# A short expert's tile, the third full tile and the two counts moved into the straight part of an attention, FFN and routed-FFN kernel

## The chip, the cores and the metric

The kernel runs on one core of one Trainium2 chip. The metric is the device time of one execution in microseconds (us), taken as the median of several runs. One core has five engines that work beside each other, each in the order of its own instructions: TensorE (PE, matmuls and transposes), VectorE (DVE), ScalarE (ACT), GpSimd (POOL) and SyncE (SP), and 16 DMA engines that the queues of SP and POOL feed. They wait for each other through semaphores.

## What is computed

The reference, cut to what matters:

```python
# q, k, v: 4 x 8 x 576 x 64, omega: 128 x 64
x = attention_by_random_features(q, k, v, omega)      # 2304 tokens x 512
x = (silu(x @ w_gate) * (x @ w_val)) @ w_out          # 512 -> 1536 -> 512

do_compute = x @ w_skip > 0                           # tokens that are routed
e_idx = np.argmax(x[do_compute] @ w_gate2, axis=1)    # one of 8 experts
for e in range(8):                                    # gate_w: softmax value of e
    h = np.maximum(xc[mask] @ w1[e], 0.0)             # 512 -> 1024
    y[mask] = gate_w[mask, None] * (h @ w2[e])        # 1024 -> 512
out[do_compute] = xc + y                              # the others: out = x
```

All is in fp32, which the kernel keeps by splitting each operand in a high and a low part and multiplying three times (high x high, low x high, high x low). For these inputs the routing sends 576 tokens to expert 1, 1135 to expert 5 and 2 to expert 4.

## The kernel before

**Order of the work.** The program is written by a small list scheduler, the class `Order` (the object `od`). A task is a Python generator that yields steps `op(engine, ns, cells it must wait for, take=(slots it needs))`. `od.run()` always takes the step that can start first by its own clock (ties by priority, the second argument of `od.add`) and emits its instructions then. So the order of instructions on each engine comes out of those estimates; on the chip every engine then follows that order, and semaphores make it wait for data. A `Cell` (`C["pick", 1]`, `C["mload", 2]`, ...) holds the time by which a step is done; slots are buffers: `hp` three PSUM banks for the up-projection of the second FFN, `y` two for its down-projection, `raw` landing buffers for weights, `ys` for copies of results.

**Stages.** Attention and the first FFN fill the program up to about 614 us and run on in part beside the routed FFN. This one works in tiles of `TS` = 288 tokens of one expert. Tiles 0 and 1 (`m` = 0, 1) are chosen early, from all but the last tokens (`early_pick`). The rest is chosen by `late_pick` (L945) after the last token is routed: a table of 64 pairs (expert, tile) with its count of tokens in each; DVE's MAX8 and FIND_INDEX8 sort out the 16 fullest (`ix[1]`, experts in `ei[1]`), and a second list (`ix[2]`, `ei[2]`) holds the "short" pairs of at most `FEW` = 64 tokens. `m2["ti"]` gets two counts: how many short pairs and how many full ones. Here they are 1 and 4 (tiles 2 to 5).

**One full tile** (`m2_tile`, L1388): `m2_up` 96 matmuls in 8 groups `fc` of 12, each into one `hp` bank (the first six of group 0 are issued ahead by `m2_head`), `m2_hidden` after each group (ACT writes the relu, L1161, DVE the low part, L1163, and the bank is free), `m2_down` 4 groups of 24 matmuls in triples (L1178 to L1180), transposed back through `yt` (L1191), scaled and added on DVE (L1202) and scattered to `out` by POOL (L1217). For the next tile it fetches the list `ids` (`m2_ids`, SP, L1042 and L1043, three landing buffers), gathers rows with POOL (`m2_gather`, L1053), transposes them (`m2_tr`, L1114; copies and low parts in L1121 to L1123), loads eight weight pieces of 0.5 MB on SP (`m2_load`, L1088) and splits each in two steps of ACT (L1099) and DVE or POOL (L1101) (`m2_split`). Weights of tile `m` lie in `W[m % 2]`.

**One short tile** (`s_*`): 64 tokens, with the tokens as the stationary side. `s_load` (L1232) and `s_split` (L1245) bring its weights into `W[1]`, `s_tokens` its list (L1256, L1257) and its rows (L1262), `s_turn` transposes them (L1293). `s_tile` runs two halves of 8 matmuls (L1319), each followed by `s_hidden` (ACT and DVE copy L1355, PE transposes L1365, ACT and DVE L1369 to L1377), then 16 matmuls (L1331) and a scatter. It holds one `hp` and both `y` banks (`s_banks`), given back by `s_back`.

**The border.** The straight program has tiles 0 and 1, the preparations of tile 2, and the loads, the first half of the split and the transposes of short tile 0. Then every engine reads the two counts into registers (`values_load`, L1510 and L1511), a nest of `tc.If(few > s)` holds up to eight short tiles (L1512), and a nest of `tc.If(cnt > n)` tiles 2 to 16 (L1525).

## Time and profile before

| | us |
|---|---|
| three runs | 860.98, 861.69, 858.26 |
| median | 860.98 |
| the profiled execution | 858.62 |
| its span from first to last instruction | 856.8 |
| PE busy in the span | 826.3 (96%) |
| DVE, ACT, POOL busy | 519.0, 446.0, 213.4 |
| mean granted clock of TensorE | 0.988 of full speed |

All times of rows are from the profiled execution and count from the start of its span. Busy time of PE is modelled from its pipelined matmuls. A timeline row gives start, duration, engine, line, operation, output and inputs, and how often it repeats; in brackets stands how long the engine was idle before and what released it. "PEldq", "SPq" and so on are the sequencers of the engines, which issue DMAs, take branches and load registers; these don't count as busy. PEclk is the clock that the throttle granted TensorE, 1.00 being full speed.

### The profile page before, as it was taken

What the parts mean: (1) busy time and instruction counts of PE and PEld (TensorE: products, weight loads), DVE (VectorE), ACT (ScalarE), POOL (GpSimd) and SP (SyncE); (2) the same over time, 40 slices, a digit from 0 to 9 for tenths busy, and PEclk for the clock granted to TensorE, in tenths of its full rate; (3) what the DMA queues carried; (4) which work ended last, traced back from release to release, by engine and by line L of the source; (5) the groups of instructions that cost most, each with busy time, mean ns of one, the idle gap of its engine ahead of it and who ended that gap; (6) DMA issues with size and microseconds to landing.
All of it is one profiled execution on the core that took longest, in us unless ns stands there. A gap on an engine that the chain in (4) does not pass through costs nothing. (4 is left out here: it accounts for less than half of the span.)

```text
span 856.8 us, 17240 instructions
## 1 busy us (share of the span) xinstructions
PE 826.3 (96%) x6221; PEld 782.1 (91%) x6221; DVE 519.0 (61%) x1477; ACT 446.0 (52%) x1162; POOL 213.4 (25%) x286
## 2 busy tenths in 40 slices
PE   9999999999999999999999999999999987999993
PEld 8989999999999999999999999999999975999993
DVE  7898877548777851832832822822567666555761
ACT  5897766337767642632632623522356255544650
POOL 4331231222222211221221212231250233113231
PEclk9999999999999999999999999999999999899997
DMA  6855862010223100200101101001285294657641
GB/s 162 239 172 178 245 195 75 1 62 27 57 62 105 39 13 2 75 1 22 55 1 37 40 1 56 7 2 50 74 252 173 71 286 151 219 159 227 197 128 31
DMA packets 77303, 84.55 MB, mean 99 GB/s; under 512 B 19549, under 2 KB 54493, under 8 KB 77200
## 3 DMA queue, kind: packets, MB, share of 16 engines
q1 hardware_dynamic: 73840, 76.23, 28.7%
q0 software_dynamic: 3360, 7.04, 2.8%
q8 instruction: 53, 0.87, 0.5%
q14 instruction: 50, 0.41, 0.2%
HBM read 71.48 MB, written 13.27 MB: 99 GB/s over the span
## 5 line engine op out<-in xcount | busy, mean ns | idle before, releaser
L669 PE MATMUL u<-xth,W 128*128 128x256 f32 x1728 | 247.1, 286 | 0.0
L669 PEld LDWEIGHTS u<-xth,W 128*128 128x128 f32 x1728 | 225.2, 190 | 5.4
L697 POOL TENSOR_TENSOR hl<-h,hh 128x256 fp32r<-128x256 f32 x108 | 82.8, 767 | 341.2 <-ACT hh L695 341.1
L669 PE MATMUL u<-xtl,W 128*128 128x256 f32 x864 | 138.8, 283 | 0.0
L669 PEld LDWEIGHTS u<-xtl,W 128*128 128x128 f32 x864 | 119.1, 192 | 0.0
L687 DVE SCALAR_TENSOR_TENSOR h<-h,u 128x256 f32<-128x256 f32 x108 | 45.3, 420 | 112.2 <-ACT h L685 111.6
L695 ACT CAST hh<-h 128x256 fp32r<-128x256 f32 x108 | 43.7, 404 | 115.0 <-DVE h L690 114.8
L690 DVE TENSOR_TENSOR h<-h,u 128x256 f32<-128x256 f32 x108 | 45.3, 419 | 73.5 <-PE u L669 72.8
L712 PE MATMUL y<-W,hh 128*128 128x512 f32 x216 | 87.4, 405 | 0.0
L713 PE MATMUL y<-W,hh 128*128 128x512 f32 x216 | 85.1, 394 | 0.0
L714 PE MATMUL y<-W,hl 128*128 128x512 f32 x216 | 84.6, 392 | 0.0
L685 ACT ACTIVATE h<-u 128x256 f32<-128x256 f32 x108 | 41.2, 381 | 83.1 <-PE u L669 80.4
L1101 DVE TENSOR_TENSOR W<-raw,W 128x512 fp32r<-128x512 f32 x108 | 73.4, 711 | 14.5 <-ACT W L1099 13.3
L1141 PE MATMUL hp<-xgt,W 128*128 128x288 f32 x546 | 77.3, 303 | 3.6 <-PEq L1512 3.6
L1141 PEld LDWEIGHTS hp<-xgt,W 128*128 128x128 f32 x546 | 75.6, 194 | 4.1 <-issue 4.0
L1099 ACT CAST W<-raw 128x512 fp32r<-128x512 f32 x112 | 64.9, 622 | 6.0 <-DMA raw<-in_moe_w_dram 5.8
L396 ACT ACTIVATE pexp<-pexp,st 128x128 f32<-128x128 f32 x184 | 58.8, 391 | 13.3 <-DVE st L389 13.0
L1178 PE MATMUL ym<-W,W 128*128 128x288 f32 x168 | 52.4, 312 | 0.0
L312 POOL TENSOR_TENSOR sq<-a 128x256 f32<-128x256 f32 x54 | 34.1, 631 | 73.1 <-DVE st L318 50.5
L360 DVE TENSOR_TENSOR th<-tp,th 64x256 fp32r<-64x256 f32 x92 | 38.8, 422 | 19.8 <-ACT th L357 17.8
L1180 PE MATMUL ym<-W,W 128*128 128x288 f32 x168 | 49.9, 297 | 0.0
L1179 PE MATMUL ym<-W,W 128*128 128x288 f32 x168 | 49.9, 297 | 0.0
(217 smaller groups left out, 1520.4 us busy)
## 6 DMA issues: line engine op xcount, KB each, us to landing
raw<-in_moe_w_dram SPq DMA_DIRECT2D x64, 512.0 KB, 4.6
scratch<-in_moe_w_out_dram SPq DMA_DIRECT2D x11, 511.8 KB, 4.2
scratch<-in_moe_w_gate_dram SPq DMA_DIRECT2D x11, 511.0 KB, 4.5
scratch<-in_moe_w_val_dram SPq DMA_DIRECT2D x11, 511.0 KB, 4.6
x2s<-x SPq DMA_DIRECT2D x9, 512.0 KB, 2.6
out_dram<-x SPq DMA_DIRECT2D x9, 512.0 KB, 3.6
a<-in_q_dram SPq DMA_DIRECT2D x26, 128.0 KB, 2.2
a<-in_k_dram SPq DMA_DIRECT2D x22, 128.0 KB, 2.2
```

The lines of the kernel that those rows point to most:

```text
L396: nc.scalar.activation(out=box["pexp"][:, h, :], in_=pj[:, h, :], func=ACTF.Exp, bias=bi[:, h:h + 1])
L669: nc.tensor.matmul(ps, lhsT=W[fc][:, 2 * n + wi, c * P:(c + 1) * P], rhs=x[:, c, :], start=(a == 0 and c == 0), stop=(a == 2 and c == 3),)
L697: nc.gpsimd.tensor_tensor(out=hl, in0=h, in1=hh.bitcast(F32), op=ALU.subtract)
L712: nc.tensor.matmul(y[n], lhsT=hh[:, s], rhs=W[fc][:, 4, :], start=(fc == 0), stop=False)
L713: nc.tensor.matmul(y[n], lhsT=hh[:, s], rhs=W[fc][:, 5, :], start=False, stop=False)
L714: nc.tensor.matmul(y[n], lhsT=hl[:, s], rhs=W[fc][:, 4, :], start=False, stop=(fc == NFC - 1))
L1099: nc.scalar.copy(blk(m, b, 0), raw[:, j, :])
L1101: (nc.vector if od.eng == "dve" else nc.gpsimd).tensor_tensor(out=blk(m, b, 1), in0=raw[:, j, :], in1=blk(m, b, 0).bitcast(F32), op=ALU.su ...
L1141: nc.tensor.matmul(hp[:, 0:TS], lhsT=blk(m, (fc // 4) * 4 + c, wi)[:, fs], rhs=m2["xt"][xi][:, c, :], start=(a == 0 and c == 0), stop=(a = ...
L1178: nc.tensor.matmul(y, lhsT=wh, rhs=hh, start=(fc == 0), stop=False)
L1179: nc.tensor.matmul(y, lhsT=wl, rhs=hh, start=False, stop=False)
L1180: nc.tensor.matmul(y, lhsT=wh, rhs=hl, start=False, stop=(fc == 7))
```

## The change

Short tile 0 and tile 2 join the straight program: `s_tile(0)`, `s_back(0)` and `m2_tile(2)` are added to `od` before the one `od.run()`, so that the scheduler lays their steps among each other. The split of the short tile's weights is whole there too (16 blocks). The weights of short tile 0 stay in `W[1]`; tile 3's loads come after the short tile's (`C["sload"]`). The list of short tile 0 and that of tile 2 are issued before the first weight piece of tile 2 (`C["slisted", 0]`, `C["listed", 2]`). `load_counts` reads the two registers when the pick is done and tile 0's up-projection too; it takes part in the schedule. The border becomes one branch with two arms, `If(few > 1)`: the arm with more short tiles, and `Else` with tiles from 3 on (`tiles()`); with `preferred_fallthrough_block=False` the code of `Else` stands right behind the branch. The scheduler's state is saved and set back so that both arms start from the same one. As tile 2 is now computed whether or not it has tokens, short pairs must not stand in the list of full ones: `late_pick` keeps the marks of all non-empty pairs in `some`, takes the full ones out, and lowers the keys of the short pairs (two more DVE operations).

```diff
--- before.py
+++ after.py
@@ -954,14 +954,17 @@
             t = yield op("dve", 130, t)
             nc.vector.tensor_tensor(out=key, in0=key, in1=tmp, op=ALU.add)
         t_k = t
-        for n, least in enumerate((0.0, float(FEW))):
+        some = m2["jts"]
+        for n, (least, at) in enumerate(((0.0, some), (float(FEW), tmp))):
             t = yield op("dve", 130, t_k if n == 0 else t)
-            nc.vector.tensor_single_scalar(out=tmp, in_=key, scalar=least, op=ALU.is_gt)
+            nc.vector.tensor_single_scalar(out=at, in_=key, scalar=least, op=ALU.is_gt)
             t = yield op("dve", 130, t)
-            nc.vector.tensor_reduce(out=m2["nt"][:, n:n + 1], in_=flat(tmp), axis=AX.X, op=ALU.add)
+            nc.vector.tensor_reduce(out=m2["nt"][:, n:n + 1], in_=flat(at), axis=AX.X, op=ALU.add)
         t = yield op("dve", 80, t)
         nc.vector.tensor_tensor(out=m2["nt"][:, 0:1], in0=m2["nt"][:, 0:1], in1=m2["nt"][:, 1:2], op=ALU.subtract)
 
+        t = yield op("dve", 130, t)
+        nc.vector.tensor_tensor(out=some, in0=some, in1=tmp, op=ALU.subtract)
         t = yield op("dve", 130, t)
         nc.vector.scalar_tensor_tensor(out=tmp, in0=tmp, scalar=-4096.0, in1=key, op0=ALU.mult, op1=ALU.add)
         t = yield op("dve", 130, t)
@@ -974,7 +977,8 @@
         )
         yield op("dve", 80, t)
         nc.vector.tensor_copy(m2["ti"], m2["nt"])
-        t = t_k
+        t = yield op("dve", 130, t_k)
+        nc.vector.scalar_tensor_tensor(out=key, in0=some, scalar=-4096.0, in1=key, op0=ALU.mult, op1=ALU.add)
         for r in range(2):
             m8 = m2["m8"][r]
             t = yield op("dve", 130, t)
@@ -1045,6 +1049,7 @@
             in_=table.rearrange("(i r p) w -> i r p w", r=3, p=SUB)[bass.ds(r, 1)].rearrange("i r p w -> p (i r) w"),
         )
         C["ids", m].t = t + 2500
+        C["listed", m].t = 0.0
 
     def m2_gather(m):
         rows = NT if m > 1 else NT - 256
@@ -1080,8 +1085,9 @@
     def m2_load(m):
 
         src, n = m2_pos(m)
+        before = {2: [C["listed", 2], C["slisted", 0]], 3: [C["sload"]]}.get(m, [])
         for i in range(8):
-            t = yield op("dma", 1456, C["pick", src], C["mload", m - 1], take=("raw",))
+            t = yield op("dma", 1456, C["pick", src], C["mload", m - 1], *before, take=("raw",))
             raw = od.got[0]
             if i == 0:
                 r = nc.sync.value_load(m2["ei"][src][0:1, n:n + 1], min_val=0, max_val=E - 1)
@@ -1156,7 +1162,8 @@
             )
 
     def m2_hidden(m, fc, hp, t):
-        t = yield op("act", 291, t, C["W2", 1, 5], *([C["h7"]] if fc == 7 else []))
+        after = [C["h7"], *([C["sdn", 0]] if m == 2 else [])] if fc == 7 else []
+        t = yield op("act", 291, t, C["W2", 1, 5], *after)
         hh, hl = m2_hid(fc, 0), m2_hid(fc, 1)
         nc.scalar.activation(out=hh, in_=hp[:, 0:TS], func=ACTF.Relu)
         t = yield op("dve", 369, t)
@@ -1232,6 +1239,11 @@
             nc.sync.dma_start(out=raw, in_=w_src(r, i))
             C["sraw", s, i].t = t + 950 + L_RAW
             C["sraw", s, i].buf = raw
+        C["sload"].t = t
+
+    def s_blk(s, i, part):
+
+        return blk(1 if s == 0 else 2, i, part)
 
     def s_split(s, first_, last):
         for b in range(first_, last):
@@ -1239,20 +1251,22 @@
 
             after = [C["so", s, int(b > 12)]] if b > 10 else []
             t = yield op(
-                "act", 520, C["sraw", s, i], C["mups", 1], C["sup", s - 1] if b < 8 else C["sdn", s - 1], *after
+                "act", 520, C["sraw", s, i], C["mups" if b < 8 else "mdown", 2 if s else 1],
+                C["sup", s - 1] if b < 8 else C["sdn", s - 1], *after
             )
             raw = C["sraw", s, i].buf
-            nc.scalar.copy(blk(1, b, 0), raw[:, j, :])
+            nc.scalar.copy(s_blk(s, b, 0), raw[:, j, :])
             t = yield op({"pool": 1225} if b in ON_POOL else {"dve": 602, "pool": 1225}, 0, t)
             (nc.vector if od.eng == "dve" else nc.gpsimd).tensor_tensor(
-                out=blk(1, b, 1), in0=raw[:, j, :], in1=blk(1, b, 0).bitcast(F32), op=ALU.subtract
+                out=s_blk(s, b, 1), in0=raw[:, j, :], in1=s_blk(s, b, 0).bitcast(F32), op=ALU.subtract
             )
             C["sw", s, b].t = t
             if j:
                 rel("raw", t, raw)
 
     def s_tokens(s):
-        t = yield op("dma", 500, C["pick", 1], C["table", NG - 1], C["gone", 0], C["sout", s - 1])
+        t = yield op("dma", 500, C["pick", 1], C["table", NG - 1], C["sout", s - 1])
+        C["slisted", s].t = 0.0
         r = nc.sync.value_load(m2["ix"][2][0:1, s:s + 1], min_val=0, max_val=NPAIR - 1)
         nc.sync.dma_start(
             out=m2["sid"][s % 2],
@@ -1278,8 +1292,8 @@
         for y in ys:
             rel("sb", od.now, y)
 
-    def s_back():
-        yield op(None, 0, take=("sb",) * 3)
+    def s_back(s):
+        yield op(None, 0, C["sdn", s], take=("sb",) * 3)
         for name, what in zip(("hp", "y", "y"), sorted(od.got, key=lambda x: x is not m2["sbank"])):
             rel(name, od.now, what)
 
@@ -1306,9 +1320,9 @@
         C["sxt", s].t = t
 
     def s_tile(s):
+        yield op(None, 0, C["mdown", 2 if s else 1], take=("ys", "ys"))
+        held = od.got
         xg = m2["sxg"]
-        yield op(None, 0, C["mdown", 1], take=("ys", "ys"))
-        held = od.got
         th = []
         for hf in range(2):
             for c in range(4):
@@ -1317,7 +1331,7 @@
                     hp = od.got[0]
                 for part in range(2):
                     nc.tensor.matmul(
-                        hp, lhsT=m2["sxt"][c // 2][:, c % 2], rhs=blk(1, 4 * hf + c, part),
+                        hp, lhsT=m2["sxt"][c // 2][:, c % 2], rhs=s_blk(s, 4 * hf + c, part),
                         start=(c == 0 and part == 0), stop=(c == 3 and part == 1),
                     )
             th.append(od.add(s_hidden(s, hf, hp, t), 0))
@@ -1329,7 +1343,7 @@
                 y = od.got[0]
             for part in range(2):
                 nc.tensor.matmul(
-                    y, lhsT=hs[:, fc], rhs=blk(1, 8 + fc, part),
+                    y, lhsT=hs[:, fc], rhs=s_blk(s, 8 + fc, part),
                     start=(fc == 0 and part == 0), stop=(fc == 7 and part == 1),
                 )
         C["sdn", s].t = t
@@ -1503,30 +1517,57 @@
         C["sup", -1].t = C["sdn", -1].t = 0.0
         od.add(s_load(0), 3)
         od.add(s_banks(), 1)
-        od.add(s_split(0, 0, 8), 5)
+        od.add(s_split(0, 0, 16), 5)
         od.add(s_tokens(0), 1)
         od.add(s_turn(0), 2)
+        od.add(s_tile(0), 1, C["sout", 0])
+        od.add(s_back(0))
+        counts = []
+
+        def load_counts():
+            yield op(None, 0, C["pick", 1], C["mups", 0])
+            for i, most in enumerate((E, 15)):
+                counts.append(nc.values_load(m2["ti"][0:1, i:i + 1], min_val=0, max_val=most))
+
+        od.add(load_counts())
+        m2_tile(2)
         od.run()
-        few = nc.values_load(m2["ti"][0:1, 0:1], min_val=0, max_val=E)
-        cnt = nc.values_load(m2["ti"][0:1, 1:2], min_val=0, max_val=15)
-        with ExitStack() as nest:
-            for s in range(E):
-                nest.enter_context(tc.If(few > s))
-                if s:
+        few, cnt = counts
+
+        cells = {k: dict(vars(c)) for k, c in C.items()}
+        state = dict(od.free), {k: list(v) for k, v in od.slots.items()}, od.now, dict(m2), list(scattered)
+
+        def tiles():
+            C["mload", 3].t = od.free["pe"] + L_LAST
+            with ExitStack() as nest:
+                for n in range(1, 15):
+                    nest.enter_context(tc.If(cnt > n))
+                    m2_tile(n + 2)
+                    od.run()
+
+        with tc.If(few > 1, preferred_fallthrough_block=False) as arms:
+            with ExitStack() as nest:
+                for s in range(1, E):
+                    if s > 1:
+                        nest.enter_context(tc.If(few > s))
+                    od.add(s_banks(), 1)
                     od.add(s_tokens(s), 1)
                     od.add(s_turn(s), 1)
                     od.add(s_load(s), 3)
-                od.add(s_split(s, 0 if s else 8, 16), 5)
-                od.add(s_tile(s), 1, C["sout", s])
-                od.run()
-        od.add(s_back())
-        od.run()
-        C["mload", 2].t = od.free["pe"] + L_LAST
-        with ExitStack() as nest:
-            for n in range(15):
-                nest.enter_context(tc.If(cnt > n))
-                m2_tile(n + 2)
-                od.run()
+                    od.add(s_split(s, 0, 16), 5)
+                    od.add(s_tile(s), 1, C["sout", s])
+                    od.add(s_back(s))
+                    od.run()
+            tiles()
+        C.clear()
+        for k, was in cells.items():
+            vars(C[k]).update(was)
+        m2.clear()
+        m2.update(state[3])
+        od.free, od.slots, od.now = state[:3]
+        scattered[:] = state[4]
+        with arms.Else():
+            tiles()
 
 
 # ---- launch: one core; inputs and outputs as the reference has them ----
```

SyncE where the pick is done, at the start of tile 1: `ids` is the list of tile 2, `sid` that of the short tile, `raw` the weight pieces of tile 2, `ix` and `ei` the indices that the pick found. Before:

```order
L1088 ISA
L1088 DMA raw<-in_moe_w_dram 128x2x512
L1042 TENSOR_LOAD ix_7890
L1042 ISA x2
L1043 ISA
L1043 DMA ids_7876<-table 96x3x2
L1088 ISA
L1088 DMA raw<-in_moe_w_dram 128x2x512
L1256 TENSOR_LOAD ix_7891
L1256 ISA x2
L1257 ISA
L1257 DMA sid_7899<-table 64x2
```

and now:

```order
L1270 TENSOR_LOAD ix_7891
L1270 ISA x2
L1271 ISA
L1271 DMA sid_7899<-table 64x2
L1046 TENSOR_LOAD ix_7890
L1046 ISA x2
L1047 ISA
L1047 DMA ids_7876<-table 96x3x2
L1093 TENSOR_LOAD ei_7893
L1093 ISA x2
L1094 ISA
L1094 DMA raw<-in_moe_w_dram 128x2x512
```

Both lists stand ahead of the first weight piece of tile 2, of which four stood ahead of the list before (the last two are shown); the register loads (L1530) stand in front of these rows.

PE in tile 1's down-projection (`ym` a `y` bank, `W` hidden values and weights), where the gathered rows of tile 2 (`xg`) are transposed for the first time. Before:

```order
L1178 MATMUL ym_8869<-W_8548,W_8816 128x288
L1179 MATMUL ym_8869<-W_8548,W_8816 128x288
L1180 MATMUL ym_8869<-W_8905,W_8816 128x288
L1114 MATMUL hp_8868<-ident,xg_7871 128x96
L1114 MATMUL hp_8868<-ident,xg_7872 128x96
L1114 MATMUL hp_8868<-ident,xg_7873 128x96
L1114 MATMUL hp_8746<-ident,xg_7871 128x96
```

and now:

```order
L1187 MATMUL ym_8869<-W_8905,W_8816 128x288
L1185 MATMUL ym_8869<-W_8548,W_8816 128x288
L1186 MATMUL ym_8869<-W_8548,W_8816 128x288
L1187 MATMUL ym_8869<-W_8905,W_8816 128x288
L1120 MATMUL hp_8868<-ident,xg_7871 128x96
L1120 MATMUL hp_8868<-ident,xg_7872 128x96
L1120 MATMUL hp_8868<-ident,xg_7873 128x96
L1185 MATMUL ym_8869<-W_8548,W_8839 128x288
```

The transposes stood behind 19 triples of the down-projection, with three chunks of 128 columns in a row; now the first chunk stands behind 4 triples, and more of tile 1's triples follow it.

PE around the short tile (`sxg` and `sxt` its rows before and after the transposes, `xgt` the transposed rows of a full tile). Before:

```order
L1293 MATMUL ym_8869<-ident,sxg 128x64 x4
L1510 TENSOR_LOAD ti
L1511 TENSOR_LOAD ti
L1512 COMPARE_AND_BRANCH
L1319 MATMUL ym_8870<-W_8649,sxt_9180 128x512 x4
L1319 MATMUL ym_8870<-W_8649,sxt_9181 128x512 x2
L1319 MATMUL ym_8870<-W_8684,sxt_9181 128x512 x2
L1319 MATMUL hp_8853<-W_8684,sxt_9180 128x512 x4
L1319 MATMUL hp_8853<-W_8751,sxt_9181 128x512 x2
L1365 MATMUL ym_8869<-ident,ys 128x128 x4
L1319 MATMUL hp_8853<-W_8751,sxt_9181 128x512 x2
```

and now, the rows around the first half of its up-projection:

```order
L1333 MATMUL hp_8853<-W_8649,sxt_9180 128x512 x4
L1333 MATMUL hp_8853<-W_8649,sxt_9181 128x512 x2
L1333 MATMUL hp_8853<-W_8684,sxt_9181 128x512 x2
L1147 MATMUL hp_8868<-xgt_7877,W_8459 128x288 x3
L1147 MATMUL hp_8868<-xgt_7877,W_8460 128x288
L1147 MATMUL hp_8868<-xgt_7877,W_8459 128x288 x3
L1147 MATMUL hp_8868<-xgt_7877,W_8460 128x288
L1147 MATMUL hp_8868<-xgt_7878,W_8459 128x288 x3
L1147 MATMUL hp_8868<-xgt_7878,W_8460 128x288
L1379 MATMUL hp_8853<-ident,ys 128x128 x4
L1147 MATMUL hp_8746<-xgt_7877,W_8460 128x288 x2
```

Register loads and branch are gone from there, and groups of tile 2 (L1147) stand between the halves and the transposes of the short tile. All stages of the short tile on PE now use one bank, `hp_8853`, and tile 2's groups alternate between `hp_8746` and `hp_8868`.

## Rows read from the trace of the kernel before

**Rows 1.** Windows: us, busy (x instructions) of each engine, PEclk, DMA share, GB/s.

```profile
690.70:712.10 21.40, 17.20 (x124) 16.94 (x124) 11.85 (x21) 10.24 (x23) 9.28 (x8) 0.92 0.80 238
712.10:725.00 12.90, 10.01 (x49) 7.20 (x47) 9.91 (x21) 8.76 (x20) 6.37 (x5) 1.00 0.57 184
...
758.90:771.20 12.30, 12.30 (x95) 12.30 (x94) 7.23 (x16) 5.95 (x13) 2.84 (x3) 1.00 0.30 90
771.20:786.70 15.50, 15.50 (x125) 15.49 (x125) 10.42 (x19) 8.60 (x19) 4.50 (x4) 1.00 0.87 274
```

**Rows 2.** Timeline of PE in tile 1's down-projection.

```profile
702.96 1.04 PE L1114 MATMUL hp<-ident,xg 96*128 96x96 f32 x7 [4.20 <-DMA xg<-x2s,ids]
```

**Rows 3.** Windows behind the two gaps of PE.

```profile
703.00:707.00 4.00, 4.00 (x22) 3.98 (x23) 2.49 (x5) 2.14 (x5) 0.26 (x1) 0.57 0.64 161
728.50:734.00 5.50, 5.43 (x22) 5.44 (x23) 0.73 (x2) 0.82 (x2) 0.59 (x1) 0.50 0.55 176
```

**Rows 4.** Timeline of SP's queue from the pick on.

```profile
679.10 2.65 SPq L1088 DMA_DIRECT2D raw<-in_moe_w_dram  x4
682.62 0.34 SPq L1043 DMA_DIRECT2D ids<-table  x1
...
694.78 21.76 SPq L1232 DMA_DIRECT2D raw<-in_moe_w_dram  x8
```

**Rows 5.** Landing of the eight lists of L1043, the longest is tile 2's.

```profile
DMA to landing us min/median/max: 1.8/2.6/7.3
```

**Rows 6.** Timeline of POOL: last scatter of tile 0, gathers of tile 2.

```profile
681.61 0.92 POOL L1217 DMA_INDIRECT out_dram<-xg,ids  x1 [0.30 <-issue]
690.68 1.43 POOL L1053 DMA_INDIRECT xg<-x2s,ids  x1 [8.14 <-DMA ids<-table]
...
695.27 1.17 POOL L1053 DMA_INDIRECT xg<-x2s,ids  x1 [0.30 <-issue]
```

**Rows 7.** Timeline of PE through the short tile to tile 2.

```profile
714.29 2.05 PE L1319 MATMUL ym<-W,sxt 128*128 128x512 f32 x8 [1.32 <-DVE sxt L1301]
...
717.55 0.60 PE L1365 MATMUL ym<-ident,ys 128*128 128x128 f32 x4
...
719.08 0.90 PE L1365 MATMUL ym<-ident,ys 128*128 128x128 f32 x4 [0.46 <-ACT ys L1355]
721.05 3.94 PE L1331 MATMUL hp<-W,h 128*128 128x512 f32 x16 [1.07 <-DVE h L1377]
728.57 1.32 PE L1141 MATMUL hp<-xgt,W 128*128 128x288 f32 x4 [3.58 <-PEq L1512]
```

**Rows 8.** PE's branches by line: count, ns min/median/max, first and last start.

```profile
L1512 PEldq COMPARE_BRANCH  x3: 92/192/3701, 713.7 to 728.2; - x3
L1525 PEldq COMPARE_BRANCH  x6: 65/74/3442, 728.4 to 845.9; - x6
```

**Rows 9.** Timeline of DVE, last search of the pick.

```profile
677.84 0.22 DVE L983 FIND_INDEX8 ix<-m,key 128x8 uint32<-128x64 f32 x1
```

**Rows 10.** Landing of the 24 gathers of L1053.

```profile
DMA to landing us min/median/max: 2.9/5.4/7.6
```

**Rows 11.** PE's register loads by line, the waits before the first included.

```profile
L1510 PEldq EVENT_SEMAPHORE  x6: 51/51/51, 712.0 to 712.5; - x6
...
L1510 PEldq TENSOR_LOAD <-ti x1: 494/494/494, 712.6 to 712.6; - x1
...
L1511 PEldq TENSOR_LOAD <-ti x1: 314/314/314, 713.2 to 713.2; - x1
```

**Rows 12.** Timeline of ACT and DVE behind one up-group of tile 2.

```profile
738.51 0.41 ACT L1161 ACTIVATE W<-hp 128x288 fp32r<-128x288 f32 x1 [0.68 <-PE hp L1141]
738.82 0.61 ACT L1099 CAST W<-raw 128x512 fp32r<-128x512 f32 x1
738.95 0.46 DVE L1163 SCALAR_TENSOR_TENSOR W<-hp,W 128x288 fp32r<-128x288 f32 x1 [0.40 <-ACT W L1161]
```

**Rows 13.** Landing of the eight weight pieces of L1232.

```profile
DMA to landing us min/median/max: 3.2/4.8/9.0
```

## The prediction

> **What bounds the kernel now.** I read the windows first, cut at the stage borders of the second FFN [rows 1]. A later tile is the yardstick: in 758.9 to 771.2 the up-projection keeps TensorE (PE) busy 12.30 of 12.30 us (95 matmuls, 0.13 us each), in 771.2 to 786.7 the down-projection and the start of the next tile 15.50 of 15.50, both at clock 1.00. Nothing but matmuls limits those two, and this change doesn't touch their number. Three stretches before them fall short: tile 1's down-projection takes 21.40 us, the short tile 12.90 with PE busy 10.01, and tile 2's up-projection begins at half the clock [rows 3].
>
> The timeline of PE then names the gaps. In tile 1's down-projection PE waits 4.20 us for the third gather of tile 2's tokens [rows 2]; behind that gap it runs 4.0 us at clock 0.57, nearly all at the lower of its two levels (1.2 of 2.4 GHz), which costs 4.0 x 0.43 = 1.7 [rows 3]. Sum 5.9, which is just 21.40 − 15.50. Why the gather is late stands in the queues: SP issued four weight pieces from 679.10, then tile 2's list at 682.62 [rows 4]; that list landed 7.3 us later where the median is 2.6 [rows 5]; GpSimd (POOL), done with its scatters at 682.53, waited 8.14 us for it and issued the third gather at 695.27 [rows 6], which landed after 702.96 − 695.27 = 7.7 us.
>
> In the short tile PE waits 1.32, 0.46 and 1.07 us, one link of its chain matmul, ScalarE (ACT), VectorE (DVE) after another, and then 3.58 us at the branch [rows 7]. PE's sequencer spent 3701 ns in one compare-and-branch, the taken `few > 1`; the loop's branches that were not taken have a median of 74 ns, and its one taken branch, at the end, 3442 [rows 8]. After the gap tile 2 begins with 5.5 us at clock 0.50: 2.75 lost [rows 3].
>
> **The change, part by part.** (a) **Lists first.** The list of the short tile and that of tile 2 go out ahead of the weight pieces of tile 2. The last search of the pick ends at 678.06 [rows 9]; of two more DVE operations of that size (0.22) one stands before it now, and the output updates of tile 0 too, so I put the indices at about 679 and tile 2's list at 679.5, on DMA queues that hold no weight piece of this tile yet: median landing 2.6 [rows 5], there by 682.1. The register loads on SP stand ahead of the lists, but wait for nothing that the pick doesn't wait for itself. POOL has its three scatters and its register loads (1 us) ahead, to 683.5, then the short tile's gather, then three of tile 2's at some 1.25 us each (1.43 and 1.17 in [rows 6]): the last issues at about 687.3 instead of 695.27. Gathers land in 2.9 to 7.6 us, median 5.4 [rows 10]: 690.2 to 694.9, likely 692.7. PE wants it earlier too: the transposes of tile 2 now stand behind 4 triples of down-matmuls instead of 19, so at 690.7 + 12 x 0.13 = 692.3, or 692.8 with (d). Stall 0 to 2.1, I take 0.5. A stall that short leaves no stretch at the lower clock in the trace before (the waits of 1.32 in [rows 7] have none behind them: 1.00 in that row of [rows 1]). Gain 5.9 − 0.5. The weight pieces of tile 2 start some 1.5 us later, which costs nothing: all were issued before the short tile's first at 694.78 [rows 4], and PE wants them from 706 on.
>
> (b) **Short tile between tile 2's groups.** Its matmuls stay: 32 at 0.246 (3.94 for 16, [rows 7]) is 7.9, with two groups of transposes of 0.60 and the 0.46 before them 9.5 of the stage's 12.9. So 3.4 can go. What is late next: tile 2's groups alternate between two PSUM banks instead of three, as the short tile keeps the third for all of its stages. A bank is free about 0.4 + 0.41 + 0.46 us after its group, by ACT and then DVE [rows 12], against 12 x 0.13 = 1.6 us of the other bank's group: 0.3 to spare. ACT works in order, and one weight cast ahead is 0.61 [rows 12]. Five groups can be hit, besides two links of the short tile's own chain, so 0 to 4 us; I take 1.2 for two collisions with a cast, and 0.5 for weight pieces (last rival) that land later than the median. Gain 3.4 − 1.7.
>
> (c) **Branch.** `few > 1` now falls through and the loop stands right behind it. On the path remain one or two untaken branches of 0.07, the bound from below; 3701 from above. With the gap goes the stretch at half rate. Gain 3.6 + 2.75 = 6.3. By the page "Runtime: NRT & Kernel Launch" of the Trainium skill, section "Instruction fetch mechanics", a taken branch to a target outside the prefetched window waits for a fetch; that fits 3701 against 74, and by it the gain would be the same 6.3.
>
> (d) **Counts early.** The register loads leave the border and stand after 18 matmuls of tile 1's up-projection. On PE's sequencer they took from 712.0 to 713.5, waits on old events included [rows 11], then hidden behind the wait of 1.32 in the short tile. Now no such wait covers them; what covers them is the matmuls that PE has queued, so 0 to 1.5; I take 0.5, since six waits of 51 ns and two loads drain a queue whose depth no row shows. ACT and DVE pay about as much, in a kind of stage where they are busy 5.95 and 7.23 of 12.30 [rows 1].
>
> The sum: 5.9 + 3.4 + 6.3 = 15.6 comes off, 0.5 + 1.7 + 0.5 = 2.7 is put on, net 12.9. Against the profiled execution (858.62, span 856.8) that gives 845.7. That execution is 2.4 under the median of the three, 860.98, and I expect the median to move alike: 848.1.
>
> **Rivals.** **Gather still late.** If the list waits behind other transfers as before (7.3 in [rows 5]) the last gather lands after 697, PE waits over 4 us and gets the slow stretch again: 5.9 comes back less the half us counted, 853.5. Against it: no weight piece of the tile is ahead of the list. **One-bank chain.** If ACT and DVE, in order and 8.76 + 5.95 us busy (ACT, [rows 1]) in the 22 of the joint stage, lose each of seven handovers a cast, 7 x 0.61 = 4.3, and a slow stretch of 1.7 follows, the price is 6.0 − 1.2: 852.9. For it speaks the margin of 0.3. **The jump isn't the gap.** The change then doesn't do what it says in (c): another gap of 3.6 and its 2.75 appear at the new border, 848.1 + 6.3 = 854.4. By the section "Control Flow Timing" of "Advanced Engine Details and Errata" in the Trainium skill, a compare-and-branch takes about 108 ns; were that all, the 3.58 us would belong to something else and stay, which is this rival. The row of 3701 ns against its own neighbours speaks against it.
>
> **Slower: the ring of weight buffers.** Tile 3's pieces are cast on ACT in the middle of tile 2's up-projection, ahead of relus that PE needs. One buffer serves in turn a piece of the short tile, another of the short tile, then tile 3's first; each turn is a landing L and about 2 us of cast and subtraction. The first of them starts at about 696.3 (694.78 and the 1.5 of (a)), so tile 3's piece is there at 696.3 + 3L + 4. Its cast stands behind the second half of the short tile's up-projection: from 690.7 + 15.5 = 706.2 on PE, 0.8 + 0.5 + 2 x 1.6 + 2.0 + 1.6 + 0.6 + 1.6 + 2.0 of groups, at 718.5. Slip 3L − 18.2: none at the median of 4.8, 8.8 at the maximum of 9.0 [rows 13]. To be slower by over 0.5% of 861 it needs 17, so L of 11.8; at L = 13 it gives 848.1 + 20.8 = 869. That is beyond any row; a slip of 3 at L = 7 isn't, and lies in the range.
>
> **How the numbers follow.** Chances: forecast 0.61, late gather 0.11, one-bank chain 0.13, jump 0.07, two or more of these together (857 to 865, within 0.5%) 0.05, slower 0.03. Range: without any of the costs 848.1 − 2.7 = 845.4, less 1.4 because the runs before spread by 3.4; upward to the three single rivals with 1 us: 844.0 to 855.5. 0.5%, 4.3 us, is about what a measurement of this kernel can tell from no change; the forecast and each rival alone are faster by more than that. Faster 0.92, same 0.05, slower 0.03.
>
> **What would show it.** (a): tile 2's list issued ahead of the weights and landing in under 3 us; PE's wait ahead of tile 2's first transposes under 2 us, not 4.20; tile 1's down-projection 15.5 to 17.5. (b): from the head of tile 2 to its last up-group some 21.5 to 23.5 with gaps of under 1 us each, those ended by ACT casts if I mis-sized them. (c): PE's `few > 1` near 0.1 us and no window at half clock in tile 2 or 3. (d): PE idle 0 to 1.5 in tile 1's up-projection. I am wrong if the border to tile 3 shows a gap of over 2 us, or if weight pieces end ACT's waits inside tile 2's up-projection for more than 3 us in sum.

## Result and the profile after

The changed kernel takes 850.12 us (median of 4, 846.94 to 852.04) against 861.06 before: ratio 0.9871 with an interval of 0.9824 to 0.9918, 10.9 us faster. A second set of six executions (below, `again`) gave 0.9884 [0.9838, 0.9931]. The forecast was 848.1, the range 844.0 to 855.5.

The profiled execution took 846.94, the fastest of the four; its span is 844.7, 12.1 less than the span before. The page's first lines:

```profile
span 844.7 us, 17205 instructions
## 1 busy us (share of the span) xinstructions
PE 822.8 (97%) x6221; PEld 778.4 (92%) x6221; DVE 517.5 (61%) x1477; ACT 446.0 (53%) x1162; POOL 215.9 (26%) x288
```

The windows that answer to [rows 1], with the same columns: tile 1's down-projection, tile 2's groups with the short tile between them, tile 2's down-projection, tile 3's up-projection.

```profile
690.90:707.30 16.40, 15.23 (x120) 14.81 (x119) 11.64 (x21) 9.86 (x22) 4.32 (x4) 1.00 0.92 274
707.30:730.10 22.80, 22.34 (x142) 19.93 (x141) 17.69 (x33) 15.94 (x36) 4.54 (x3) 1.00 0.72 235
730.10:745.40 15.30, 15.30 (x123) 15.13 (x121) 11.74 (x23) 8.39 (x19) 6.57 (x6) 1.00 0.57 195
746.40:758.70 12.30, 12.30 (x95) 12.30 (x94) 5.38 (x13) 4.42 (x10) 6.59 (x7) 1.00 0.56 182
```

The clock is 1.00 in all of them, where [rows 3] had 0.57 and 0.50. What is left of PE's waits stands in its timeline, four rows for [rows 2] and [rows 7]:

```profile
693.46 0.30 PE L1120 MATMUL hp<-ident,xg 96*128 96x96 f32 x1 [0.74 <-DMA xg<-x2s,ids]
694.19 0.30 PE L1120 MATMUL hp<-ident,xg 96*128 96x96 f32 x1 [0.43 <-DMA xg<-x2s,ids]
...
711.52 1.73 PE L1147 MATMUL hp<-xgt,W 128*128 128x288 f32 x11 [0.28 <-DVE W L1170]
...
726.58 2.11 PE L1345 MATMUL hp<-W,h 128*128 128x512 f32 x8 [0.17 <-DVE h L1391]
```

SP and POOL, for [rows 4] and [rows 6]: the lists now precede the weights, and tile 2's last gather is issued at 687.86 instead of 695.27 (`sid` is the short tile's list, `ids` tile 2's).

```profile
676.87 0.56 SPq L1271 DMA_DIRECT2D sid<-table  x1
678.67 0.36 SPq L1047 DMA_DIRECT2D ids<-table  x1
680.63 9.92 SPq L1094 DMA_DIRECT2D raw<-in_moe_w_dram  x6
...
699.20 14.62 SPq L1239 DMA_DIRECT2D raw<-in_moe_w_dram  x8
```

```profile
684.00 0.98 POOL L1276 DMA_INDIRECT sxg<-x2s,sid  x1 [0.31 <-issue]
...
687.86 0.97 POOL L1058 DMA_INDIRECT xg<-x2s,ids  x1 [0.30 <-issue]
```

PE's branches by line, for [rows 8] (L1548 is `few > 1`, L1542 the loop):

```profile
L1548 PEldq COMPARE_BRANCH  x1: 95/95/95, 746.1 to 746.1; - x1
L1542 PEldq COMPARE_BRANCH  x5: 65/68/3597, 746.3 to 833.5; - x5
```

### The profile page after: what moved, and what is told of

Same layout as the page of the kernel before. It is cut to its first block, busy times and chain, and to the rows that moved or that the text cites. A ratio compares the mean times of both kernels' runs of the same rounds, so it can differ in the third digit from the quotient of the medians.

```text
span 844.7 us, 17205 instructions
## 1 busy us (share of the span) xinstructions
PE 822.8 (97%) x6221; PEld 778.4 (92%) x6221; DVE 517.5 (61%) x1477; ACT 446.0 (53%) x1162; POOL 215.9 (26%) x288
## 5 line engine op out<-in xcount | busy, mean ns | idle before, releaser
L1147 PE MATMUL hp<-xgt,W 128*128 128x288 f32 x546 | 76.2, 297 | 0.3 <-DVE W L1170 0.3
L1147 PEld LDWEIGHTS hp<-xgt,W 128*128 128x128 f32 x546 | 73.7, 188 | 0.9 <-DVE W L1170 0.5
```

What stands on the lines that cost most here:

```text
L1147: nc.tensor.matmul(hp[:, 0:TS], lhsT=blk(m, (fc // 4) * 4 + c, wi)[:, fs], rhs=m2["xt"][xi][:, c, :], start=(a == 0 and c == 0), stop=(a = ...
```

## Experiments

Times are medians. The kernel before was run beside each set of experiments, with medians of 861.05 (`again`, `tr_later`, `jump`, `lists_late`), 860.15 (`ids_first`, `branch_only`, `apart`, `raw_late`) and 861.42 (`jump_quiet`, `apart3`, `counts_late`, `best`). A profile shows one execution, which need not lie near the median: it took 851.6 in `again`, 857.79 in `jump`, 858.45 in `ids_first`, 866.62 in `apart` and 855.94 in `raw_late`. The runs of the kernel before vary from 853.65 to 865.5 themselves, partly ahead of the changed place: a waiting PE row at 670.00 us in the trace before (transposes of tile 0's results, 0.79 us of wait) stands between 670.4 and 677.5 in the others. Where I compare traces, I count from that row to the end of the span: 186.8 us before, 174.3 after.

**again**: the changed kernel once more.

> The changed kernel once more, for its spread: its four runs lie between 846.9 and 852.0 us with mean clocks from 0.995 down to 0.989, and 0.006 of 850 us is the whole 5 us. Theory: in some executions the third gather of tile 2 lands later than in the profiled one, PE's wait ahead of tile 2's first transposes (1.2 us there) grows past some point and a stretch at half clock follows. Then these runs spread again over 4 to 6 us around 849 to 851. Rival: the spread belongs to the chip and the kernel before has the same.

851.07 (849.65 to 851.6); the kernel before spread wider beside it (853.65 to 864.83), as the rival has it. From the row at 670 on it took 175.9 in its profile, 1.6 more than the first; the rest of its 4.5 us was lost earlier. So my reason for the spread fell: there was no wait for the gather here at all. Instead there are two others, in the timelines of ACT and of PE:

```profile
687.63 0.41 ACT L1168 ACTIVATE W<-hp 128x288 fp32r<-128x288 f32 x1 [1.19 <-PE hp L1147]
692.36 0.41 ACT L1168 ACTIVATE W<-hp 128x288 fp32r<-128x288 f32 x1 [4.32 <-remote]
...
708.94 1.14 ACT L1258 CAST W<-raw 128x512 fp32r<-128x512 f32 x2 [2.00 <-DMA raw<-in_moe_w_dram]
```

```profile
693.31 1.87 PE L1147 MATMUL hp<-xgt,W 128*128 128x288 f32 x12 [0.93 <-DVE W L1170]
...
715.67 1.87 PE L1147 MATMUL hp<-xgt,W 128*128 128x288 f32 x12 [1.93 <-DVE W L1170]
```

ACT stood 4.32 us in tile 1's up-projection, and 0.93 of it reached PE. The row names no engine for it. This trace lacks some semaphore records (it has 984 of the semaphore that PE's up-groups raise, the first has 1005), but one that it holds, at 692.34, stands 0.02 us ahead of ACT's start, as those at 686.01 and 687.61 stand ahead of the two relus before. So ACT most likely waited for PE's signal, and not for its own instructions, and that signal came 3.1 us after the end that the trace models for the group (689.20). `tr_later` (below) has a stop of the same kind, and there the row names PE:

```profile
693.45 0.41 ACT L1168 ACTIVATE W<-hp 128x288 fp32r<-128x288 f32 x1 [3.95 <-PE hp L1147]
```

Why the signal came late isn't shown. A full load of the DMA engines alone doesn't make it so: their share was 1.04 in `again` from 688.0 to 692.4, and 1.05 in the same stretch of the changed kernel's first profile, which has no such stop.

Later the casts of the short tile's weights waited for them (2.00 us and two more), and the first relu of tile 2's groups stands behind six such casts in ACT's order, so that PE waited 1.93. That the casts are the cause is argued from this order, not shown.

**tr_later**: tile 2's first transposes wait for a column group of tile 1.

```diff
-            after = [C["mups", m - 1]] + ([C["mdn", m - 1, TRC[c]]] if TRC[c] >= 0 else []) if m else []
+            after = [C["mups", m - 1]] + ([C["mdn", m - 1, max(TRC[c], 0 if m == 2 else -1)]] if TRC[c] >= 0 or m == 2 else []) if m else []
```

> The transposes of tile 2's rows wait for the first column group of tile 1's down-projection, as in the kernel before, instead of standing behind its fourth triple. If the early place is what costs (1.2 us of wait in the profile, and a slow stretch in some runs), PE's wait there goes, the profiled run comes to about 845.7, and the median to 846 to 847 with a spread of 1 to 2 us. If the gather is late by more than that, or the spread has another source, the median stays at 849 to 851.

853.03, ratio to before 0.9917 [0.9888, 0.9946], so no gain over `again`, but 2.0 more. The wait for the gather is gone from its trace, but PE waits 1.66 us behind ACT at the end of tile 1's up-projection, 1.49 behind the casts, and 1.35 in tile 3, with no releaser named. Taken alone, this place wasn't what held the kernel.

**jump**: the same program with the arms laid out the other way.

```diff
-        with tc.If(few > 1, preferred_fallthrough_block=False) as arms:
+        with tc.If(few > 1) as arms:
```

> The same program, but the arm with further short tiles stands right behind the branch, so that the arm that is run is reached by a taken branch. Theory (the gap is the jump): PE's few > 1 takes 3.4 to 3.7 us, PE is idle about 3.5, tile 3 starts at half clock for some 5.5 us, 2.75 lost: 6.3 us slower than the changed kernel, some 856. Rival (the gap belonged to something else at the old border, a compare and branch is 0.1 us): within 1 us of the changed kernel.

860.83, ratio to before 1.0013 [0.9983, 1.0043]: 9.8 us above `again`, and the whole gain is gone. The jump is the gap, but dearer than I took it from [rows 8]. By line, in PE's timeline, in SP's, and as a window that begins in the gap:

```profile
L1548 PEldq COMPARE_BRANCH  x1: 6840/6840/6840, 747.7 to 747.7; - x1
```

```profile
754.71 2.52 PE L1147 MATMUL hp<-xgt,W 128*128 128x288 f32 x9 [6.46 <-issue]
```

```profile
745.70 2.55 SPq L1094 DMA_DIRECT2D raw<-in_moe_w_dram  x4
```

```profile
750.50:760.50 10.00, 5.79 (x24) 5.80 (x25) 0.60 (x2) 0.82 (x2) 3.23 (x4) 0.50 0.65 221
```

SP had passed the border and issued four weight pieces of tile 4 between 745.70 and 748.25, around PE's branch at 747.7.

**jump_quiet**: `jump` without those four pieces (tile 4 computes with old weights).

```diff
-            nc.sync.dma_start(out=raw, in_=w_src(r, i))
+            if m != 4 or i > 3:
+                nc.sync.dma_start(out=raw, in_=w_src(r, i))
```

> The kernel of the run jump, without the first four weight pieces of tile 4 (2 MB; tile 4 then computes with old weights). In jump these were issued at 745.7 to 748.3, and PE's taken branch at 747.7 took 6840 ns; in the kernel before no piece was issued within 5 us of the branch, which took 3701. Theory: the branch waits for a fetch that shares the DMA engines with the weights, so it takes 3.4 to 4 us here, and the run is some 3 us and a part of the half clock faster than jump (median 860.8), 855 to 858. Rival: the longer branch belongs to the target's distance; it stays at 6 to 7 us, and the time at 859 to 861.

855.59, 5.2 less than `jump`. The branch takes 3520 ns and PE's gap 3.14:

```profile
L1549 PEldq COMPARE_BRANCH  x1: 3520/3520/3520, 749.9 to 749.9; - x1
```

```profile
753.64 3.70 PE L1148 MATMUL hp<-xgt,W 128*128 128x288 f32 x16 [3.14 <-issue]
```

So a taken branch costs PE some 3.5 us where no weights are on the way and 6.8 behind 2 MB of them. Both jump from the same place to the same arm, and the rival falls. "Runtime: NRT & Kernel Launch" of the Trainium skill, section "Instruction fetch mechanics", says that a taken branch to a target outside the prefetched pages must first fetch it by DMA; the two runs agree with that.

**lists_late**: the changed kernel without the lists' precedence.

```diff
-        before = {2: [C["listed", 2], C["slisted", 0]], 3: [C["sload"]]}.get(m, [])
+        before = {3: [C["sload"]]}.get(m, [])
```

> The two lists go back behind four and five weight pieces of tile 2; the rest of the change stays. The scheduler then puts tile 2's transposes back behind some 20 triples. Theory: tile 2's list lands over 5 us after its issue, the third gather lands at about 701 to 703, PE waits 3 to 4.5 us and runs a stretch at half clock: 4 to 6 us slower than the changed kernel, 853 to 856. Rival (the list is late for another reason, or the gathers wait for POOL): the same time as the changed kernel within 1 us.

855.32, as the theory had it: 4.3 above `again`. PE waits twice for the gather, although the transposes stand some 20 triples later, and 704 to 712 runs at clock 0.79:

```profile
704.48 0.30 PE L1120 MATMUL hp<-ident,xg 96*128 96x96 f32 x1 [2.10 <-DMA xg<-x2s,ids]
...
706.22 0.80 PE L1120 MATMUL hp<-ident,xg 96*128 96x96 f32 x7 [1.44 <-DMA xg<-x2s,ids]
```

**ids_first**: the kernel before, with tile 2's list ahead of its weights and nothing else.

```diff
+        C["listed", m].t = 0.0
...
-            t = yield op("dma", 1456, C["pick", src], C["mload", m - 1], take=("raw",))
+            t = yield op("dma", 1456, C["pick", src], C["mload", m - 1], *([C["listed", 2]] if m == 2 else []), take=("raw",))
```

> The kernel before with one part of the change: tile 2's list is issued ahead of the tile's weight pieces. The scheduler then puts its first transposes behind one triple of tile 1's down-projection. Theory: the list lands in about 2 to 3 us, the third gather at 688 to 693, PE waits 0 to 2 us there instead of 4.2, no slow stretch there: 4 to 6 us faster than before. The gap at the branch and the half clock behind it stay. Rival: other waits take the place (instruction fetch or weights that land later), gain under 2 us.

856.18 against 860.15, 4.0 faster [0.9923, 0.9971]. The wait for the gather is 1.63 us, the one at the branch stays:

```profile
696.41 0.30 PE L1115 MATMUL hp<-ident,xg 96*128 96x96 f32 x1 [1.63 <-DMA xg<-x2s,ids]
```

```profile
729.36 3.05 PE L1142 MATMUL hp<-xgt,W 128*128 128x288 f32 x13 [3.01 <-PEq L1513]
```

**branch_only**: the kernel before, with short tile 0 ahead of one branch in its old place, and the arm with tiles 2 and on right behind that branch.

```diff
-            for s in range(E):
-                nest.enter_context(tc.If(few > s))
...
+        od.add(s_split(0, 8, 16), 5)
+        od.add(s_tile(0), 1, C["sout", 0])
+        od.run()
...
+        with tc.If(few > 1, preferred_fallthrough_block=False) as arms:
```

> The kernel before with another part of the change alone: short tile 0 is computed without a branch around it, in its old place, and behind it stands one branch with two arms whose arm that is run (tiles 2 and on) follows directly. PE's order of matmuls is that of before. Theory: PE's gap of 3.58 and the 2.75 of half clock behind it go: 6 us faster than before, 854 to 856, the gather's gap stays. Rival: the gap stays within 1 us of 3.58 since the border itself (register loads, waits) makes it: under 1 us.

858.25 against 860.15, ratio 0.9974 [0.9945, 1.0003]: 1.9, with an interval from -0.3 to 4.7, so not 6, and not clearly more than nothing. The branch is cheap, as in the changed kernel, and the gap is gone:

```profile
L1528 PEldq COMPARE_BRANCH  x1: 95/95/95, 728.4 to 728.4; - x1
```

The half clock isn't. The stretch behind the border is nearly gone, but one now falls into the end of the short tile, behind the waits of its chain (1.24, 0.46 and 1.10, about those of [rows 7]):

```profile
724.00:728.40 4.40, 3.29 (x9) 2.56 (x9) 3.89 (x7) 3.09 (x7) 0.81 (x1) 0.68 0.28 96
728.50:734.00 5.50, 5.50 (x35) 5.09 (x34) 2.28 (x4) 1.41 (x3) 0.79 (x1) 0.96 0.85 281
```

So in this trace, at least, the slow stretch that I booked wholly to the jump isn't the jump's alone. From the short tile's first matmul to the end it is 4.1 us shorter than the trace before. The other 2.1 were lost ahead of that, in tile 1's down-projection, where the gathers came later and the half clock lasted longer than in [rows 3]:

```profile
705.93 1.38 PE L1114 MATMUL hp<-ident,xg 96*128 96x96 f32 x7 [4.00 <-DMA xg<-x2s,ids]
```

```profile
704.00:712.00 8.00, 6.07 (x29) 6.03 (x30) 2.88 (x6) 2.63 (x6) 1.78 (x2) 0.57 0.65 189
```

The edit changes nothing there, so this part is the spread of executions and no price of the branch.

**apart** and **apart3**: the changed kernel with the short tile ahead of tile 2's groups. In `apart3` it also takes its result buffers only when all of tile 1 is copied out.

```diff
         od.add(load_counts())
+        od.run()
         m2_tile(2)
         od.run()
```

```diff
-        yield op(None, 0, C["mdown", 2 if s else 1], take=("ys", "ys"))
+        m = 2 if s else 1
+        yield op(None, 0, C["mdown", m], *[C["back", m, dc] for dc in range(4)], take=("ys", "ys"))
```

> The changed kernel, but with the short tile ahead of tile 2's groups instead of between them. Theory (the short tile's waits were 2.9 us with nothing between, and all its stages share one bank now): 3 to 5 us slower than the changed kernel, 854 to 856, with waits of 0.4 to 1.4 us between its stages. Rival (interleaving only moves the waits into tile 2's groups, as in the profile of the changed kernel's second execution, 1.93 + 0.17 us): within 1 us of the changed kernel.

> As apart, but the short tile takes its buffers for results only when all four column groups of tile 1 are copied out, so its stages on PE use three banks, in the order of the kernel before; tile 2's groups follow behind it. Theory: the 11 us that apart lost against the changed kernel were mostly the single bank; here the short tile's waits are those of before (1.3, 0.5 and 1.1), the stage costs 2.4 to 3.4 us more than interleaved, 853 to 855. Rival: without interleaving any order loses as much as apart (862): then it is half clock or weights that come late.

`apart` took 862.16, above the 854 to 856 expected, `apart3` 854.82: with the three banks of before the short tile's waits are about those of [rows 7], and not interleaving costs 3.9 against `counts_late` (850.96), which was measured beside it, or 3.8 against `again`. Three of PE's waits in `apart`, and the clock:

```profile
719.01 3.08 PE L1333 MATMUL hp<-W,sxt 128*128 128x512 f32 x8 [2.97 <-DVE sxt L1315]
723.05 1.11 PE L1379 MATMUL hp<-ident,ys 128*128 128x128 f32 x4 [0.97 <-DVE ys L1371]
725.66 3.78 PE L1333 MATMUL hp<-W,sxt 128*128 128x512 f32 x8 [1.49 <-DVE ys L1385]
```

```profile
720.00:730.00 10.00, 6.98 (x17) 4.27 (x16) 4.88 (x8) 3.87 (x10) 2.86 (x2) 0.50 0.62 200
```

and in `apart3`:

```profile
713.27 2.12 PE L1334 MATMUL ym<-W,sxt 128*128 128x512 f32 x8 [1.24 <-DVE sxt L1315]
718.13 0.90 PE L1380 MATMUL ym<-ident,ys 128*128 128x128 f32 x4 [0.46 <-ACT ys L1370]
720.15 5.07 PE L1346 MATMUL hp<-W,h 128*128 128x512 f32 x14 [1.12 <-DVE h L1392]
```

```profile
720.00:730.00 10.00, 9.85 (x50) 8.75 (x51) 6.94 (x14) 6.33 (x14) 2.75 (x3) 0.83 0.78 253
```

The single bank, then, is a choice that the schedule fell into: `s_tile` takes both `ys` buffers as soon as PE is done with tile 1, before ACT has copied its fourth column group, and that group keeps its `y` bank until the short tile is through. The copy in the changed kernel's trace:

```profile
731.14 0.41 ACT L1194 COPY ys<-ym 128x288 f32<-128x288 f32 x1
```

This is 24 us after tile 1's last down-matmul. With the short tile laid among tile 2's groups, most of what the single bank costs is hidden: PE's waits there are 0.28 and 0.17 in the changed kernel's profile.

**raw_late**: the scheduler assumes that the short tile's pieces land 2 us later.

```diff
-            C["sraw", s, i].t = t + 950 + L_RAW
+            C["sraw", s, i].t = t + 950 + 3 * L_RAW
```

> The changed kernel with one number changed: the scheduler takes the short tile's weight pieces to land 2 us later (measured 4.0 to 6.3 us where it assumed some 2), so ACT has 3 of their casts, not 6, ahead of the first relu of tile 2's groups. If those casts in order hold up the relus (PE waits of 1.5 to 1.9 us behind DVE in two of three profiles), the waits go and the time falls by 1 to 2 us, to 849 to 850. If the weights come late for PE anyway, the short tile's matmuls wait instead: no change.

852.12, ratio 0.9909 [0.9875, 0.9942], against the 849 to 850 expected. No wait behind a cast is left among tile 2's groups, but no time was won: in this execution the gather was late by 0.71 and 1.01 us, and 702 to 712 ran at 0.83. The traces of `jump` and `counts_late` have no such wait either, so this run neither shows the casts as its cause nor rules them out.

**counts_late**: the register loads at the border.

```diff
+        m2_tile(2)
+        od.run()
         od.add(load_counts())
-        m2_tile(2)
         od.run()
```

> The changed kernel with the register loads at the border, behind tile 2's down-projection, instead of in tile 1's up-projection. Theory: PE's sequencer takes some 1.5 us for them where nothing covers it, and the branch follows: 0.5 to 2 us slower than the changed kernel, 851.5 to 853. Rival: PE has matmuls queued, no difference.

850.96, as `again` and below the 851.5 to 853 expected. PE has one wait of 1.38 at the border, while its sequencer is in the register loads and the branches (747.7 to 749.6):

```profile
749.64 2.66 PE L1147 MATMUL hp<-xgt,W 128*128 128x288 f32 x18 [1.38 <-DVE xg L1209]
```

So a loss of that size is there in the trace, but too small for these times to show.

**best**: `tr_later`, `raw_late` and the later taking of `ys` together.

> The changed kernel with the three things that the runs so far point to: tile 2's transposes behind the first column group (no wait for the gather), the short tile's weights taken to land 2 us later, and its buffers for results taken only when tile 1 is copied out, so that its stages use three banks. If each wait in the profile of the changed kernel is worth its length: 1.2 + 0.3 + 0.2, and 1.5 to 2 in executions like the second one, 847 to 849.5. If the waits only move on (instruction fetch on ACT, weights), 850 to 853.

847.84 (846.21 to 849.59), ratio 0.9852 [0.9833, 0.9872], 13.6 faster than before. All its executions lie below those of `again`, though beside other runs of the kernel before. Neither of the first two parts gained anything alone, and the third was not run alone in the interleaved order, so which of them wins isn't shown. PE is busy all the time in the two stages of the change, in a profile that took 172.3 from the row at 670 on, 2.0 less than the changed kernel's:

```profile
692.00:708.00 16.00, 16.00 (x128) 15.99 (x128) 11.87 (x22) 10.36 (x23) 2.89 (x3) 1.00 0.96 295
708.00:731.00 23.00, 23.00 (x154) 21.34 (x153) 19.52 (x38) 16.71 (x39) 10.33 (x9) 1.00 0.84 262
```

One wait of 0.88 stands behind them, at 734.98.

## Why the prediction was right, and where it was off

The sum of 12.9 held for the profiled pair (186.8 − 174.3 = 12.5 from the row at 670 on). The median lies 2.0 above the forecast: 1.2 of it in the profiled pair (846.94 against 845.7: some 0.4 each in the sum, ahead of the row at 670 and outside of the span), 0.8 because the profiled execution lies further below its median (3.2) than that of before (2.4). By stages the pair gives 4.4 up to tile 2's head, 9.0 from there to tile 2's down-projection (711.28 to 743.12 before, 707.29 to 730.12 after), and 0.8 lost again behind it. I had 5.4 for the first and 8.0 for the second, so two errors of 1.0 offset each other, and that the sum came out so close is in part luck. By steps:

- **(a) lists first**: the mechanism is shown by `ids_first` (4.0) and `lists_late` (4.3). Tile 2's list went out at 678.67 (I had 679.5) and landed after 1.9 us, the last gather was issued at 687.86 (687.3). It landed at about 694.1, after 6.3 us rather than the median 5.4: all four gathers that were issued from 684 to 688, among the weight pieces, took 6.2 to 6.8, so the median was the wrong size for that place. PE waited 1.17 where I had taken 0.5, inside the bounds of 0 to 2.1. That such a wait leaves no slow stretch held in the first profile, and behind 1.71 in `apart3`, but not in `raw_late`, behind 1.72. Gain some 4.4 (711.28 − 690.51 before against 707.29 − 690.88, from its down-projection's start to tile 2's head), expected 5.4; two thirds of the difference is the longer wait, the rest I can't name.
- **(b) between the groups**: PE's waits there are 0.28 + 0.17, not 1.2, in the profiled execution; in `again` they are 2.1. `apart3` puts the worth of interleaving at 3.8, above my 1.7 net: besides waits of 2.8 its trace has a stretch at half clock behind them, where I took waits that short to leave none.
- **(c) branch**: the sign was right, and the mechanism, that the gap is the taken branch, is shown by `jump` and `jump_quiet`. The size of 6.3 depends on the place. Alone, in the old place, it is 1.9 by the times (`branch_only`, -0.3 to 4.7) and 4.1 in the one trace, for the half clock came there without the gap too; at the new border a jump would cost 9.8 (`jump`), as four weight pieces are in flight there. I had priced the jump by [rows 8] at a place without that traffic. The median of 74 that I read there is that of all six branches of the line, the taken one included; the untaken ones took 65 to 78, which changes nothing.
- **(d) counts**: cost nothing visible in PE's timeline of the changed kernel (expected 0.5): from the row at 670 to tile 1's down-projection PE needs 20.5 us in both traces. At the border it would be 1.38.
- **Rivals**: the late gather, the jump that isn't the gap, and the ring of buffers didn't come. Short pieces landed after 4.0 to 6.3 us, and tile 3's casts held nothing up for long. The one-bank chain is real, as `apart` shows, and is covered by the interleaving; it comes through in part in executions like `again`. ACT's stops of 4 us (`again`, `tr_later`) may account for some of what the median lacks; that isn't shown.

Taken one at a time, the lists give 4.0, the branch 1.9 and the interleaving, by its removal, 3.8: 9.7, which within the spread is the 10 to 11 that they give together. Without the fall-through, though, the gain is 0, since the jump at the new border is dearer than the one at the old.

## What to carry to other kernels

Put small transfers that start a chain (lists, indices) on the queue ahead of bulk transfers, and look where a taken branch stands: price it by what the DMA engines carry at the place where it will stand, not where it stands now. A stretch at half clock need not belong to the last gap before it: here one gap was removed, and a stretch came behind other waits (`branch_only`). When two stages are laid among each other, follow each buffer that the second one takes early: here a result of the first one kept a bank for 24 us.

## What the runs showed of the hardware

A taken branch on PE took 3437 to 3977 ns where no weight pieces had just been issued and 6840 behind 2 MB of them; the other branches of these lines took 65 to 203. On the other engines the branch itself stays short (53 to 72 ns in `jump`), and the stop comes behind it. ACT in `jump`, the taken branch and, by its first start, the next one:

```profile
L1548 ACTq COMPARE_BRANCH  x1: 55/55/55, 747.2 to 747.2; - x1
```

```profile
L1542 ACTq COMPARE_BRANCH  x5: 34/38/50, 752.4 to 843.0; - x5
```

In the changed kernel both stand at 745.7. ACT stood for 4 us in straight code in two traces (4.32 in `again`, 3.95 in `tr_later`), most likely for a signal of PE that came 3.1 and 3.9 us after the modelled end of its matmuls; why stays open.
